# Linear attention, top-2 MoE and GLU in one kernel: remainder tokens of k and v in 1024-byte pieces, token numbers in the one-hots, two weight splits and the quarter list moved forward

## The chip, the cores and the metric

The kernel runs on one core of a Trainium2 chip, in one launch. The metric is device time in microseconds, as the median of several runs; lower is better. Engines are named as the profile names them: PE (matrix products), DVE (VectorE), ACT (ScalarE), POOL (GpSimd) and SP (the queue that issues most transfers).

## The reference

Three layers run one behind the other on 2304 tokens (4 batches of 576) of width 512 (8 heads of 64).

```python
kv = einsum('bhsd,bhse->bhde', k, v)            # 64 x 64 for each batch and head
out = einsum('bhsd,bhde->bhse', q, kv)
x = out / sqrt(mean(out * out, -1) + 1e-6) * g_norm     # then [2304, 512]

noisy = x @ w_gate + log1p(exp(x @ w_noise)) * noise    # 8 experts
top2, top2_w = two largest of noisy, softmax over the two
y[mask] += top2_w * (relu(x[mask] @ w1[e]) @ w2[e])     # F = 1024

result = (sigmoid(y @ m2_gate) * (y @ m2_val)) @ m2_out # 1536 wide, float64 weights
```

## The kernel before

**Attention.** A batch has 576 tokens: 512 "main" tokens, four neighbouring ones on each of 128 partitions (`R = 4`, pieces of 1024 bytes), and 64 remainder tokens (`SR`). `load_main` brings half of a batch's heads of k, v or q in one DMA of 512 KB; `load_rem` brings the remainder of one tensor of one batch, one token on a partition, in 512 pieces of 256 bytes (128 KB). k's remainder of two batches shares a tile; v's has one tile for each batch with zeros in the other half, so that the product over 128 partitions takes this batch alone. All these loads stand in program order in SP's queue, batch by batch: k and v of the first four heads, the remainders, k and v of the other heads, the noise, q. The small loads of `g_norm`, `w_gate` and `w_noise` are issued by ACT.

`kv_a(b)` makes the 64 x 64 products: for each of four head pairs, five steps (`R` main ones and the remainder) of two matmuls. It ends in a copy on DVE into `kvbd[b]`. `kv_b` transposes it, and `kv_c` multiplies by the gate weights times g_norm (`gwb`, which DVE makes in `early`, line 311, from `wcat` and `gcol`), so that `kvbd[b]` gives a tile's output and its gate logits in one product. For batch 0 this is done in two halves, in an order on PE that is written out by hand with filler matmuls (`warm`). Then a loop over 18 tiles of 128 tokens (`q_transpose`, `attend`) runs with `kv_a` to `kv_c` of batches 1 to 3 in it (`hooks`).

**Routing.** Tiles form four groups (`GROUPS`). `route(g)` is a generator, stepped by `advance` and `step`: it makes the norm, the logits, the two best experts (`oh`, `km`, `mk`), the rank in the expert by products on PE (`prk`), slot numbers (`sb`, `rm`), and one-hots for a list of tokens: `ohs` of the place in a block (128 wide, one instruction for each tile and choice, line 539) and `ovs` of the block (one instruction for the group, line 541, and one that multiplies it by the token numbers `tokid`, line 543). Of `ohs`, all of group 0, the second choices of groups 1 and 2 and three of the last group's five second choices are made by POOL, the others by DVE. A sum of their products is the list of tokens for each block: `pfirst` over the first two groups gives the first two blocks of expert 0 (`lsa`, two gathers on POOL), `plist` over all groups gives everything (`lsb`). `lsq` holds the same list for gathers by quarter rows, which experts 1 to 7 use.

**Experts.** The first 256 tokens of expert 0 are computed while the last two groups are still being routed: `h_first(0..3, 0)` for the hidden layer, `y_step(0, 0)` and `y_step(0, 1)` for its output. Between them `work()` splits the next piece of an expert's weights into a high part (ACT, line 644 or 647) and a low part (DVE, line 645 or 648); which `step` and which `work()` stands where is written by hand. After the list, POOL gathers blocks 2 to 4 of expert 0, DVE scales them (`xs`), PE transposes them, ACT and DVE make `xh` and `xl`, and `h_first(0..3, 1)` starts. From there expert follows expert: PE does three products for each exact one, DVE and ACT split weights and hidden values, POOL gathers and scales the next expert's rows (lines 714, 720 and 733). The GLU follows, in a table of steps made at build time. SP and POOL keep program order; PE and DVE have the order of the text where a `with in_order` says so, and a list scheduler's order elsewhere.

## Time and profile before

| | |
|---|---|
| median of 3 runs | 944.24 us (944.13 to 947.38) |
| the profiled execution | 937.66 us, of which 935.9 us are the span of instructions |
| PE busy in the span | 909.1 us (97%) |
| DVE, ACT, POOL busy | 682.3, 439.6, 383.6 us |
| transferred | 213.92 MB, 229 GB/s on average |

All rows below are of one profiled execution, which was 6.6 us shorter than the median of the plain runs. Times count from the start of the span. A share of busy time is an average over stages, so stages are looked at one by one. "Busy" of PE counts overlapping matmuls once, and its idle time is printed with the name of what ended it.

### The profile page before, as it was taken

How to read it: one execution, taken by the hardware profiler on the slowest of the kernel's cores; microseconds unless marked ns; L12 is line 12 of the kernel's file. 1: busy time of each engine (PE TensorE's matmuls, PEld its weight loads, DVE VectorE, ACT ScalarE, POOL GpSimd, SP SyncE). 2: the span in 40 equal slices, each digit the busy share in tenths (PEclk: the TensorE clock that was granted, in tenths of full speed). 3: DMA queues.
4: the chain of work that ended last, by engine and by line, in shares of the span. 5: the costliest groups of instructions: out<-in, count | busy, mean ns of one | idle time of the engine just before them, and what ended most of it. 6: DMA issues, size and time to landing. Idle time of an engine off the chain costs nothing.

```text
span 935.9 us, 14318 instructions
## 1 busy us (share of the span) xinstructions
PE 909.1 (97%) x5157; PEld 788.7 (84%) x5157; DVE 682.3 (73%) x1025; ACT 439.6 (47%) x659; POOL 383.6 (41%) x378
## 2 busy tenths in 40 slices
...
GB/s 263 290 257 216 188 216 279 259 257 274 262 188 234 185 221 194 207 206 216 225 155 141 140 251 215 217 333 222 171 266 263 244 253 252 350 269 201 217 249 98
DMA packets 134379, 213.92 MB, mean 229 GB/s; under 512 B 20384, under 2 KB 65952, under 8 KB 134304
## 3 DMA queue, kind: packets, MB, share of 16 engines
...
q14 instruction: 34, 0.28, 0.1%
...
## 4 chain that ended last, share of the span: by engine, by line
PE 58%; DVE 5%; DMA 4%; ACT 2%; issue 2%; SPq 1%; POOL 0%; DVEq 0%; ACTq 0%
PE py L817 15%; PE ph L774 14%; PE pga L1174 8%; PE poa L1353 7%; PE pgc L1174 4%; PE poc L1353 3%; PE pgb L1174 2%; PE pout L1323 2%; PE pob L1353 2%; DMA xturn<-yg 1%; DMA yg<-ybuf,slot 1%; DVE wt L994 1%; DMA lw<-wbuf 1%; DMA yg<-xturn 1%; DVE xf L1072 1%
## 5 line engine op out<-in xcount | busy, mean ns | idle before, releaser
L714 POOL DMA_INDIRECT xg<-xbuf,lsq x132 | 152.8, 1158 | 51.2 <-issue 30.9
L994 DVE TENSOR_TENSOR wt<-lw,wt 128x512 fp32r<-128x512 f32 x84 | 69.9, 837 | 35.7 <-ACT wt L993 33.6
L778 ACT ACTIVATE hh<-ph 128x624 fp32r<-128x624 f32 (+1 forms) x60 | 41.4, 694 | 95.7 <-PE ph L774 93.9
L779 DVE SCALAR_TENSOR_TENSOR hl<-ph,hh 128x624 fp32r<-128x624 f32 (+1 forms) x60 | 48.7, 811 | 48.2 <-ACT hh L778 47.0
L714 POOL DMA_INDIRECT yg<-ybuf,slot x36 | 39.0, 1084 | 77.6 <-issue 57.7
L733 POOL TENSOR_TENSOR xg<-xg 128x512 f32<-128x512 f32 x33 | 36.5, 1107 | 40.3 <-DMA xg<-xbuf,lsq 35.2
L763 ACT ACTIVATE xh<-xT 128x512 fp32r<-128x512 f32 (+3 forms) x40 | 21.1, 543 | 66.6 <-DVE xT L760 65.4
L993 ACT ACTIVATE wt<-lw 128x512 fp32r<-128x512 f32 x84 | 49.9, 621 | 0.0
L1211 POOL TENSOR_TENSOR qt<-qv 128x512 f32<-128x512 f32 x12 | 19.7, 1642 | 68.9 <-DVE qv L1198 37.2
L1188 ACT ACTIVATE q<-pga 128x1024 f32<-128x1024 f32 x24 | 24.6, 1027 | 44.8 <-PE pga L1174 43.5
L764 DVE TENSOR_TENSOR xl<-xT,xh 128x512 fp32r<-128x512 f32 (+3 forms) x40 | 24.9, 634 | 27.0 <-ACT xh L763 27.0
L695 POOL COPY seen<-hh 128x1 f32<-128x1 f32 x42 | 16.8, 401 | 65.7 <-ACT hh L778 65.5
L774 PE MATMUL ph<-xh,w_3h 128*128 128x312 f32 (+2 forms) x128 | 39.3, 307 | 1.6 <-DVE hl L779 0.9
L774 PE MATMUL ph<-xh,w_3l 128*128 128x312 f32 (+2 forms) x128 | 39.3, 307 | 1.5 <-DVE w_3l L645 1.5
L774 PE MATMUL ph<-xl,w_0h 128*128 128x312 f32 (+2 forms) x128 | 39.1, 313 | 1.3 <-DVE xl L764 1.3
L822 ACT ACTIVATE yo<-py 128x512 f32<-128x512 f32 (+1 forms) x40 | 23.5, 588 | 35.6 <-PE py L817 32.7
L774 PE MATMUL ph<-xh,w_1l 128*128 128x312 f32 (+2 forms) x128 | 39.2, 307 | 0.7 <-DVE w_1l L645 0.7
L774 PE MATMUL ph<-xh,w_0l 128*128 128x312 f32 (+2 forms) x128 | 39.6, 312 | 0.3 <-PEq L852 0.3
L774 PE MATMUL ph<-xh,w_0h 128*128 128x312 f32 (+2 forms) x128 | 39.6, 312 | 0.0
L774 PE MATMUL ph<-xh,w_1h 128*128 128x312 f32 (+2 forms) x128 | 39.2, 306 | 0.0
L774 PE MATMUL ph<-xl,w_2h 128*128 128x312 f32 (+2 forms) x128 | 39.1, 306 | 0.0
L774 PE MATMUL ph<-xh,w_2h 128*128 128x312 f32 (+2 forms) x128 | 39.1, 306 | 0.0
...
## 6 DMA issues: line engine op xcount, KB each, us to landing
...
```

The lines of the kernel that those rows point to most:

```text
L714: nc.gpsimd.indirect_dma_start(out=x, out_offset=None, in_=src, in_offset=bass.IndirectOffsetOnAxis(ap=ix, axis=0))
L733: eng.tensor_mul(xv, xv, x[:, :, 128:, None].to_broadcast([128, 4, KD, 32]))
L764: nc.vector.tensor_sub(XL[e, s][:, :, a:z], pt[:, :, o:o + z - a], XA[e, s][:, :, a:z].bitcast(FT))
L774: nc.tensor.matmul(ph, w[:, c, j], x[e, s][:, c, :], start=(n == 0), stop=(n == 3 * KD - 1))
L778: nc.scalar.activation(hh, ph, AF.Relu)
L779: nc.vector.scalar_tensor_tensor(hl, ph, 0.0, hh.bitcast(FT), op0=OP.max, op1=OP.subtract)
L817: nc.tensor.matmul(py[0:m], x[:, f % 2, t], w[:, f % 2, :], start=(n == 0), stop=(n == 3 * FC - 1))
L993: nc.scalar.activation(hi, src, AF.Copy)
L994: nc.vector.tensor_sub(lo, src, hi.bitcast(FT))
L1174: nc.tensor.matmul(ps[:, j, 0:HT[c]], w[:, a, k, s], x[:, k, :], start=(first and i == 0), stop=(i == 5), skip_group_check=not first)
L1188: nc.scalar.activation(q[name], src, AF.Copy)
L1353: nc.tensor.matmul(ps[:, j, 0:HT[c]], w, g[x][1][:, f, :], start=(first and u + f + i == 0), stop=(u == FP3 - 1 and f + i == 3), skip_grou ...
```

## The change

Six things are changed.

1. `load_rem` brings k's and v's remainder as 16 pieces of four neighbouring tokens for each head: partition 16 h + i holds tokens 4 i to 4 i + 3 of head h, in 128 pieces of 1024 bytes. A head's tokens now stand on 16 partitions only, so masks are needed: `kown` (two tiles, zeroed once) gets the 32 partitions of a head pair by four copies a batch, and `vown` is v times a 0/1 column (`own`) for even and for odd heads, two instructions a batch. DVE does these for batch 0 and POOL for batches 1 to 3. `kv_a` then runs four remainder steps of two matmuls for each head pair instead of one.
2. `load_qrem` puts the two batches of q's remainder on even and odd partitions; `attend` takes every second column of the transposed tile. The pieces stay at 256 bytes.
3. `gcol`, `w_gate` and `w_noise` are issued by SP, behind k and v of batch 0.
4. The token number is multiplied into `ohs` as a second operation of the same instruction; the separate product on `ovs` is dropped, and the last group's second choices move from POOL to DVE.
5. The splits of w1 pieces 1 and 3 of expert 0 stand before the `h_first` that they used to stand behind.
6. The quarter list is made directly behind the whole list.

```diff
-    krem, qrem = (wt([128, B // 2, H, D], FT, f"{nm}rem") for nm in "kq")
+    kown = [wt([128, HP, R * D], FT, f"kown{i}") for i in range(2)]
+    qrem = wt([128, B // 2, H, D], FT, "qrem")
...
+    krem, vown = wt([128, B, R * D], FT, "krem"), []
+    own = cst.tile([128, 2], FT, name="own")
...
-    def load_rem(dst, src, b):
-        nc.sync.dma_start(dst[64 * (b % 2):64 * (b % 2) + 64],
-                          hbm(src, b * H * S * D + SM * D, [[D, SR], [S * D, H], [1, D]]))
+    def load_rem(b):
+        vown.append(et([128, 2, R * D], FT, f"vown{b}"))
+        nc.sync.dma_start(krem[:, b], hbm(k, b * H * S * D + SM * D, [[S * D, H], [R * D, SR // R], [1, R * D]]))
+        nc.sync.dma_start(vown[b][:, 1], hbm(v, b * H * S * D + SM * D, [[S * D, H], [R * D, SR // R], [1, R * D]]))
+
+    def load_qrem(b):
+        nc.sync.dma_start(qrem[b % 2::2, b // 2], hbm(q, b * H * S * D + SM * D, [[D, SR], [S * D, H], [1, D]]))
...
-    for s in range(2):
-        nc.scalar.dma_start(gcol[64 * s:64 * s + 64, :], hbm(g_norm, 0, [[1, 64], [1, 1]]))
-    nc.scalar.dma_start(wcat[:, :, 0:E], w_gate.rearrange("(c p) e -> p c e", p=128))
-    nc.scalar.dma_start(wcat[:, :, E:2 * E], w_noise.rearrange("(c p) e -> p c e", p=128))
+    nc.sync.dma_start(gcol, hbm(g_norm, 0, [[0, 2], [1, 64], [1, 1]]))
+    nc.sync.dma_start(wcat[:, :, 0:E], w_gate.rearrange("(c p) e -> p c e", p=128))
+    nc.sync.dma_start(wcat[:, :, E:2 * E], w_noise.rearrange("(c p) e -> p c e", p=128))
...
     def kv_a(b, pairs=(0, HP)):
         a, z = pairs
+        for hp in range(a, z):
+            p = slice(32 * hp, 32 * hp + 32)
+            (nc.gpsimd if b else nc.vector).tensor_copy(kown[b % 2][p, hp], krem[p, b])
+        for s in range(2) if not a else ():
+            (nc.gpsimd if b else nc.vector).tensor_scalar(vown[b][:, s], vown[b][:, 1], own[:, s:s + 1], None,
+                                                          op0=OP.mult)
         pk = pa([128, z - a, 128], "pkv")
         for hp in range(a, z):
-            for r in range(R + 1):
+            for r in range(2 * R):
...
-                        (krem[:, b // 2, 2 * hp + s, :], vrem[b][:, 2 * hp + s, :])
+                        (kown[b % 2][:, hp, d], vown[b][:, s, d])
...
-                eng = nc.gpsimd if j and (g != len(groups) - 1 or i < 3) or not g else nc.vector
-                eng.tensor_scalar(ohs[:, i, j], i128[:, 0:128], rm[:, i, j:j + 1], None, op0=OP.is_equal)
+                eng = nc.gpsimd if j and g != len(groups) - 1 or not g else nc.vector
+                eng.tensor_scalar(ohs[:, i, j], i128[:, 0:128], rm[:, i, j:j + 1], tokid[:, t0 + i:t0 + i + 1],
+                                  op0=OP.is_equal, op1=OP.mult)
...
-                nc.vector.tensor_mul(ovs[:, :n], ovs[:, :n], tokid[:, t0:t1, None, None].to_broadcast(shp))
...
+        work()
         step(third)
-        step(last, 2)
-        work()
-        step(last)
+        step(last, 3)
         h_first(0, 0)
     work()
     step(third)
     step(last, 4)
     step(third, 2)
-    step(last)
+    work()
     h_first(1, 0)
-    step(last, 3)
+    step(last, 4)
     step(third)
-    work()
     h_first(2, 0)
...
         for blk in range(AB, NB):
             gather(0, blk)
+        lsf = sml.tile([128, NB * E], HF, name="lsf")
+        nc.vector.tensor_copy(lsf, pl)
+        psq = pa([128, 4, NB * E], "psq")
+        for b in range(4):
+            nc.tensor.matmul(psq[:, b], sel[:, b], lsf, start=True, stop=True)
+        nc.vector.tensor_scalar(lsq, psq, quarter, 4.0 * TOK, op0=OP.add, op1=OP.add)
```

What that makes of the order is shown at two places. The first is SP's queue at the start of the program. Before, two k remainders (batches 0 and 1) and one of v stand between the two halves of batch 0's k and v (a name's number tells tiles apart):

```order
L218 DMA k_128<-in_k_dram 128x4x256
L218 DMA v_130<-in_v_dram 128x4x256
L222 DMA krem<-in_k_dram 64x8x64 x2
L222 DMA vrem_156<-in_v_dram 64x8x64
L218 DMA k_129<-in_k_dram 128x4x256
L218 DMA v_131<-in_v_dram 128x4x256
```

Now:

```order
L221 DMA k_128<-in_k_dram 128x4x256
L221 DMA v_130<-in_v_dram 128x4x256
L226 DMA krem<-in_k_dram 128x1x256
L227 DMA vown_169<-in_v_dram 128x1x256
L221 DMA k_129<-in_k_dram 128x4x256
L221 DMA v_131<-in_v_dram 128x4x256
L257 DMA gcol<-in_g_norm_dram 128x1x1
L258 DMA early<-in_moe_w_gate_dram 128x4x8
L259 DMA early<-in_moe_w_noise_dram 128x4x8
```

The remainder of batch 1 has left this place, and the three small loads of `gcol` and the gate weights (the tile `early`) have come in behind the second half of k and v. On DVE, the first instructions that wait for a load stand like this before (`kvbd` is the tile of the 64 x 64 products):

```order
L311 TENSOR_SCALAR early<-early,gcol 64x4x16 x2
L278 TENSOR_SCALAR ident<-jp 128x128
L280 TENSOR_SCALAR tri<-jp 128x128
L288 TENSOR_SCALAR sel<-sel 128x512
L355 COPY kvbd_250<-pkv 64x2x64 x2
L372 COPY kvbd_250<-pgw 128x2x32
```

Now:

```order
L349 COPY kown_152<-krem 32x256 x4
L215 TENSOR_SCALAR jown<-jown 128x2
L282 TENSOR_SCALAR ident<-jp 128x128
L217 TENSOR_SCALAR own<-jown 128x2
L284 TENSOR_SCALAR tri<-jp 128x128
L351 TENSOR_SCALAR vown_169<-vown_169,own 128x256
L292 TENSOR_SCALAR sel<-sel 128x512
L351 TENSOR_SCALAR vown_169<-vown_169,own 128x256
L315 TENSOR_SCALAR early<-early,gcol 64x4x16 x2
L365 COPY kvbd_256<-pkv 64x2x64 x2
L382 COPY kvbd_256<-pgw 128x2x32
```

The masks of batch 0 have come in ahead, and `early`, which waits for the gate weights, still stands ahead of the first copy of `kvbd`.

The second place is DVE around the whole list (`lsb`), where `w_0_1l` to `w_0_3l` are the low parts of expert 0's w2 pieces. Before:

```order
L541 TENSOR_TENSOR ohv<-i_226,sb 128x10x40
L539 TENSOR_SCALAR ohv<-i_226,rm 128x128 x6
L556 TENSOR_TENSOR tw<-tw,dn 128x5
L548 SCALAR_TENSOR_TENSOR slot<-sb,rm 128x10
L539 TENSOR_SCALAR ohv<-i_226,rm 128x128
L543 TENSOR_TENSOR ohv<-ohv,tokid 128x10x40
L554 TENSOR_SCALAR dn<-dn 128x5
L648 TENSOR_TENSOR w_0_1l<-raw,w_0_1h 128x1024
L1520 TENSOR_SCALAR lsb<-plist 128x40
L555 RECIPROCAL tw<-dn 128x5
L648 TENSOR_TENSOR w_0_2l<-raw,w_0_2h 128x1024
L556 TENSOR_TENSOR tw<-tw,dn 128x5
```

Now:

```order
L553 TENSOR_TENSOR ohv<-i_232,sb 128x10x40
L550 TENSOR_SCALAR ohv<-i_232,rm,tokid 128x128 x6
L559 SCALAR_TENSOR_TENSOR slot<-sb,rm 128x10
L550 TENSOR_SCALAR ohv<-i_232,rm,tokid 128x128 x4
L567 TENSOR_TENSOR tw<-tw,dn 128x5
L659 TENSOR_TENSOR w_0_2l<-raw,w_0_2h 128x1024
L1529 TENSOR_SCALAR lsb<-plist 128x40
L1533 CAST lsf<-plist 128x40
L659 TENSOR_TENSOR w_0_3l<-raw,w_0_3h 128x1024
L1537 TENSOR_SCALAR lsq<-psq,quarter 128x160
```

The product by `tokid` is gone, ten one-hots of the last group stand where seven stood, one more split (`w_0_2l`) stands ahead of `lsb`, and the quarter list (`lsf`, `lsq`) has moved up to it.

## Rows read from the trace of the kernel before

**Rows 1.** Busy time by stage; columns: stretch, engines' busy us, PEclk, DMA share, GB/s.

```profile
20.00:54.00 34.00, 29.83 (x408) 27.34 (x409) 16.72 (x56) 21.84 (x52) 4.21 (x4) 1.00 1.10 295
...
136.00:536.00 400.00, 397.93 (x2261) 359.20 (x2260) 306.80 (x435) 161.65 (x239) 195.75 (x199) 1.00 0.66 216
```

**Rows 2.** Timeline of PE: start us, us, instruction; in brackets the idle time before.

```profile
7.12 0.69 PE L352 MATMUL pkv<-v,k 128*64 128x64 f32 x16 [0.62 <-DMA v<-in_v_dram]
...
20.60 1.35 PE L410 MATMUL po<-kvbd,qT 128*128 128x160 f32 x8
...
48.37 0.69 PE L352 MATMUL pkv<-v,k 128*64 128x64 f32 x16
48.88 0.29 PE L352 MATMUL pkv<-vrem,krem 128*64 128x64 f32 x4
```

**Rows 3.** Waits of PE, 18 to 70 us: us in total, times, longest.

```profile
PE pkv L352 <- DMA v<-in_v_dram: 3.0, 2, 1.6
PE pkv L352 <- PE pqT L395: 0.9, 1, 0.9
PE prk L497 <- DVE mk L492: 0.8, 1, 0.8
PE pfirst L1432 <- POOL ohv L539: 0.6, 2, 0.4
```

**Rows 4.** DMA view, 0 to 54 us: GB/s in 40 slices, then queues (packets, MB, share).

```profile
GB/s 0 9 292 338 280 155 83 375 353 323 349 349 352 289 225 335 337 345 336 203 284 338 257 133 149 338 344 329 350 347 350 297 178 344 325 354 338 244 203 291
...
q10 hardware_dynamic: 1216, 0.03, 1.6%
```

**Rows 5.** Timeline of DVE, the first kv product.

```profile
9.44 0.52 DVE L311 TENSOR_SCALAR early<-early,gcol 64x64 f32<-64x64 f32 x2 [5.92 <-DMA vrem<-in_v_dram]
...
11.21 0.59 DVE L355 COPY kvbd<-pkv 64x128 f32<-64x128 f32 x2 [0.68 <-PE pkv L352]
```

**Rows 6.** Timeline of PE, the end of attention.

```profile
69.56 3.60 PE L1482 MATMUL warm<-qT 128*128 128x512 f32 x8
```

**Rows 7.** Groups of instructions of POOL, 0 to 110 us.

```profile
L539 POOL TENSOR_SCALAR ohv<-i,rm 128x128 f16<-128x128 f16 x21 | 17.5, 846 | 19.2 <-DVE rm L530 14.8 <-DVE ohv L541 4.4
```

**Rows 8.** Timeline of DVE, the routing of the last group.

```profile
78.31 1.28 DVE L645 SCALAR_TENSOR_TENSOR w_1l<-raw,gcol,w_1h 128x1024 fp32r<-128x1024 f32 x1 [1.25 <-ACT w_1h L644]
...
94.71 0.56 DVE L543 TENSOR_TENSOR ohv<-ohv,tokid 128x400 f16<-128x400 f16 x1
```

**Rows 9.** Timeline of DVE, the list and the first split behind it.

```profile
97.25 0.20 DVE L1520 TENSOR_SCALAR lsb<-plist 128x40 int32<-128x40 f32 x1 [0.77 <-PE plist L1432]
...
117.09 3.73 DVE L645 SCALAR_TENSOR_TENSOR w_0l<-raw,gcol,w_0h 128x1024 fp32r<-128x1024 f32 x1 [0.18 <-ACT w_0h L644]
```

**Rows 10.** Waits of PE, 70 to 150 us.

```profile
PE ph L774 <- DVE w_3l L645: 1.5, 1, 1.5
PE py L817 <- DVE hl L779: 1.4, 1, 1.4
...
PE plist L1432 <- POOL ohv L539: 1.3, 1, 1.3
PE ph L774 <- DVE hl L779: 0.9, 1, 0.9
PE ph L774 <- DVE w_1l L645: 0.7, 1, 0.7
```

**Rows 11.** Timeline of PE, the second half of expert 0.

```profile
109.47 0.43 PE L774 MATMUL ph<-xl,w_0h 128*128 128x368 f32 x1 [1.06 <-DVE xl L764]
...
110.08 0.51 PE L774 MATMUL ph<-xl,w_0h 128*128 128x368 f32 x1
...
113.80 0.33 PE L774 MATMUL ph<-xh,w_0l 128*128 128x368 f32 x1
```

**Rows 12.** Timeline of POOL, gathers behind the list.

```profile
107.97 0.94 POOL L714 DMA_INDIRECT xg<-xbuf,lsq  x1 [2.94 <-DVE lsq L1540]
...
117.65 2.08 POOL L720 TENSOR_TENSOR xs<-xg 128x512 f32<-128x512 f32 x2
```

37 lines of the change are left out of this document (15 added, 22 removed).

## The prediction

> **What bounds the kernel now.** I read the busy time by stage first. From 136 us to 536 us PE is busy 397.93 of 400 us [rows 1], and behind the routing of the last tokens no instruction is changed, so that the rest moves as a block: only the first 136 us can gain or lose. In the attention stage, 20 to 54 us, PE is busy 29.83 of 34 us while the DMA engines are full (share 1.10) [rows 1]. So two resources are near their limit there, and the change gives to one (loads) and takes from the other (PE). The timeline of PE shows the first tile's product at 20.60 us and the kv product of batch 3 running without a gap from 48.37 us [rows 2]; the waits of PE show what stops it: 3.0 us for v in two waits and 0.9 us at the start of batch 1's kv product, which I also take for a load, then 0.8 us for a mask and 0.6 us for POOL's one-hots [rows 3]. The DMA view shows a plateau of some 350 GB/s with dips to 155 and 83 (6.8 to 9.5 us) and 133 to 149 (31 to 34 us) where 256-byte pieces are moved [rows 4]. After attention, the view that counts is the chain from the last group's routing to the list, `lsb`, at 97.25 us, and from there to the second half of expert 0.
>
> **1. Loads.** The 38 slices of 1.35 us from 2.7 us on average 293 GB/s; at 350 they would be over 8.4 us sooner [rows 4]. Eight of the twelve remainder loads get large pieces, two pairs of q's keep theirs; I take 5 us as gained on the last load. That alone is no time: PE waits only 3.0 + 0.9 us for loads [rows 3], and no more than that can come back.
>
> **2. The start.** The gate weights go behind 4 x 512 KB + 2 x 128 KB = 2.36 MB, 6.7 us at 350 GB/s, from 2.7 us on: 9.4 us. Their 1152 small pieces cost 11.4 ns each (1.6% of 54 us x 16 engines over 1216 packets [rows 4]), 0.8 us over 16 engines. The lag from last byte to reader is about 1.4 us: 1.05 MB from 2.7 us ends at 5.7, and the first product starts at 7.12 [rows 2]. So DVE can begin `early` near 11.7 us instead of 9.44, and the first `kvbd` copy, in order behind it, comes near 12.3 instead of 11.21 [rows 5]: +1.1. The first half's added matmuls lie beside this wait; the second half's (0.8, below) are on the path; the 0.9 us wait falls away. The first tile comes 1.0 us later. Bounds: -0.9 if the gate weights are no later, +4 if they land 3 us later than taken.
>
> **3. PE.** 16 records of a main pair take 48.88 - 48.37 = 0.51 us, 4 of the remainder a quarter of it, 0.13 [rows 2]. The remainder becomes 16: +0.38 for a pair, 1.5 us a batch, 4.6 us for batches 1 to 3. Against that fall the waits for v (3.0), for the mask and for POOL (0.8 and 0.6) [rows 3], since the same scheduler now puts the mask ahead of a copy and two products by `tokid` leave DVE: -4.4. I take a further 0.4 off for those two products. End of attention on PE, 69.56 us now [rows 6]: +1.0 + 4.6 - 4.4 - 0.4 = **+0.8**. The masks on POOL, six instructions of 256 columns a batch, lie between half and twice the 0.85 us that POOL's one-hot of 128 columns takes [rows 7]; near it they are 5 us a batch, and POOL is busy 4.21 of these 34 us [rows 1], so I take nothing; without that cover, batch 1 alone could cost 2 us, since its remainder lands closest to its use. Bounds of this part: -3 (PE finds time for the matmuls in waits) to +4.
>
> **4. The list.** DVE is the bound from 74 to 97 us; I sum its queue. Gone: 1.25 us of waiting for `w_1h` [rows 8], because the split now stands earlier; 0.77 us of waiting for `plist` [rows 9], whose last factor came from POOL (PE waits 1.3 us for it [rows 10]); two `tokid` products of 0.5 [rows 8]. Added: three one-hots, 0.5; one more split ahead of `lsb` in the new order, 1.2 (as the 1.28 of [rows 8], less overlap); 0.4 for a norm that ACT now does behind a split. Sum -0.9. PE's own waits for `w_3l` and `w_1l`, 1.5 + 0.7 [rows 10], go too, but hide behind the list: PE ends its first blocks sooner and waits for the gathers. Behind the gathers, five small counting instructions stand ahead of `xl` on DVE now (+0.5), and `lsq` no longer does (-0.4). Second half of expert 0, first `xl` product at 109.47 [rows 11]: **-0.8**. Bounds: -2.0 (a wait of PE was the bound) to +0.5 (the extra split costs what the rest gives).
>
> **5. The clock.** Matmuls there go 0.51 us long at 110.08 and 0.33 us at 113.80 [rows 11]: PE had waited several times from 106 us, and for 3.4 us the granted clock is at the lower of its two levels; 11 matmuls lose 0.15 each, 1.7 us. PE will idle longer ahead of this point, so the low stretch should come earlier and lie half beside the idle time: **-0.8**. Bounds: -1.7 (all beside) to +1.7 (two such stretches).
>
> **6. Behind the list.** POOL waits 2.94 us for `lsq`, starts expert 1's quarter gathers at 107.97, and scales two blocks at 117.65 for 2.08 us [rows 12]. In that time DVE's split `w_0l` takes 3.73 us [rows 9] instead of 1.28, as if it stood behind POOL; the next loads wait for its buffer, and PE pays 0.9 and 1.4 us later [rows 10]. With `lsq` ready some 9 us sooner, POOL starts these gathers when it ends the others, about 3 us earlier, and the scaling is over as the split begins: **-1.9** of the 2.3. Bounds: -2.3 to +0.5 (POOL meets another instruction instead).
>
> Sum: +0.8 - 0.8 - 0.8 - 1.9 = -2.7. The profiled execution took 937.66 us, so 935.0; the median of plain runs stood 6.6 us above it, so 944.24 - 2.7 = **941.5 us**. 0.5% is 4.7 us, about what a measurement of this kernel can tell from no change.
>
> **A rule that speaks against it.** In this kernel's rows every load has 64 or 128 as its outermost count, and the queue keeps all 16 engines at work (share 1.10 [rows 1]). The new k and v remainders have 8 heads outermost. The Trainium skill (DMA: Bandwidth & Descriptors, "Why a DMA increments its semaphore by 16 and not by 1") says that a transfer is split over the largest number of engines up to 16 that divides both sides' outermost counts; by that, these eight loads run on 8 engines, and `gcol`, with 2 outermost, on 2. No row of before shows such a load; worked out from rows it is the second rival.
>
> **Rivals.** *Attention follows its loads* (faster): PE's added matmuls find their place in waits that the names of the rows do not show, and the end of attention moves by -3 instead of +0.8. For it: PE is 4.2 us idle in 20 to 54 us and the loads come 5 us sooner. Against it: the gap-free stretches of PE. 941.5 - 3.8 = 937.7. *Half the engines*: a remainder pair is 256 pieces; an engine moves 1024 bytes in 47 ns at 350 GB/s over 16, so the pair takes 32 x 47 ns = 1.5 us of 8 engines instead of 0.75 of 16, 0.75 us a batch for all that queues behind. If that and POOL's masks behind it keep the 3.0 us of waits for v alive, the time is 944.5. *Late gate weights* (slower): every tile stands behind `kvbd` of batch 0, and that on DVE behind `early`. If small pieces at the end of a full queue land 4 us later than I took (15.7 instead of 11.7), the first tile is 4 us later, all of attention with it, and the time is 945.5; it decides from 2.7 us on. The old trace has a sign of it: a wait of 5.92 us for loads ahead of `early` [rows 5]. That the change would not do what it says is seen in one place: `lsb` stands behind one more split, which is in the sum.
>
> **How the numbers follow.** The forecast, 0.44; attention follows its loads, 0.26; half the engines, 0.17; late gate weights, 0.13. The range 936.5 to 946.5 takes in all four centres and leaves the last tenth on either side to sums of bounds. Faster by over 0.5% (under 939.5): nearly all of the first rival and a little of the forecast, 0.28. Slower by over 0.5% (over 949.0): half of the late weights, 0.07. Within: 0.65.
>
> **What would show it.** Right: no wait of PE for v from 20 to 54 us, GB/s without the dips at 7 to 9 and 31 to 34 us, the first tile near 21.6 us, filler at the end of attention near 70.4, `lsb` near 97.1 with no wait for POOL, quarter gathers near 105, `w_0l` under 2 us, and no waits of PE of 0.9 and 1.4 us near 125 and 135 us. Wrong: `early` on DVE past 14 us; waits of PE for POOL's masks in batch 1; a start of the second half of expert 0 at or behind 109.5; POOL's scaling beside another split.

## The result and the profile after

| | |
|---|---|
| before, median of 6 runs | 945.81 us (944.13 to 948.82) |
| changed, median of 6 runs | 957.81 us (954.84 to 961.88) |
| ratio | 1.0132, 95% interval 1.0103 to 1.0162 |
| forecast | 941.5 us, range 936.5 to 946.5 |
| profiled execution, changed | 960.37 us, of which 958.1 us are the span |

The changed kernel is 1.3% slower, some 12.5 us. The profile of before is of an execution that was short for its kernel, so the two spans (958.1 and 935.9) are 22 us apart, and only part of that is the change. Where the 22 us arise is read from places that both programs pass, each a row of the timeline of PE (the list: of DVE):

| place, us from the start | before | changed | difference |
|---|---|---|---|
| first tile's product | 20.60 | 23.53 | +2.9 |
| end of attention on PE | 69.56 | 79.33 | +9.8 |
| list `lsb` | 97.25 | 106.17 | +8.9 |
| second half of expert 0, first `xl` product | 109.47 | 120.35 | +10.9 |
| expert 1, first hidden product | 147.07 | 158.20 | +11.1 |
| GLU, first `pgv` product | 533.79 | 545.11 | +11.3 |
| GLU, first `pga` product | 572.09 | 594.22 | +22.1 |

By the first product of expert 1 some 11 us are lost, most of them by the end of attention, and they stay up to the GLU. The other 10.8 us lie between `pgv` and `pga` (49.1 us instead of 38.3); run 1 below shows 47.8 us there for the unchanged kernel, so they belong to the execution.

Busy time by stage of the changed kernel, with the columns of [rows 1]:

```profile
20.00:54.00 34.00, 29.90 (x412) 27.52 (x410) 13.30 (x29) 18.69 (x43) 14.41 (x22) 0.95 1.07 300
...
70.00:110.00 40.00, 37.11 (x247) 30.40 (x248) 32.33 (x118) 19.13 (x37) 15.17 (x18) 0.91 0.42 139
110.00:136.00 26.00, 20.66 (x105) 18.98 (x103) 12.71 (x26) 8.85 (x11) 21.76 (x21) 0.80 0.70 208
```

and the two middle stages of before:

```profile
70.00:110.00 40.00, 33.32 (x235) 26.72 (x234) 31.77 (x108) 16.38 (x29) 17.61 (x20) 1.00 0.59 186
110.00:136.00 26.00, 23.66 (x125) 21.94 (x124) 20.92 (x23) 13.19 (x15) 18.57 (x19) 0.93 0.74 224
```

In attention PE is as busy as before (29.90 us of 34, 29.83 in [rows 1]), and its clock is 0.95 instead of 1.00; run 17 below, a later profile of the unchanged kernel, has 0.95 there too. From 70 to 110 us it is 0.91 and from 110 to 136 us 0.80, where before had 1.00 and 0.93. The DMA engines are at 0.42 instead of 0.59 from 70 to 110 us, since the list and its gathers come later.

**The start.** SP's queue of the changed kernel (start us, us on the queue):

```profile
5.10 3.72 SPq L258 DMA_DIRECT2D early<-in_moe_w_gate_dram  x1
8.87 1.33 SPq L259 DMA_DIRECT2D early<-in_moe_w_noise_dram  x1
...
12.21 1.13 SPq L221 DMA_DIRECT2D q<-in_q_dram  x2
```

The load of `w_gate` keeps the queue for 3.72 us, those of `w_noise` and the noise behind it 1.33 us each, so that q of batch 0 is issued at 12.21 us. In the profile of before q went at 9.88, and SP's queue had stood for 3.3 us in two waits that the profile puts down to `gcol`'s load on ACT's queue (3.2 us in run 2, 3.3 in run 4 below): the queue was held in both orders. The DMA view, 0 to 54 us in 40 slices of 1.35 us, has the hole that follows:

```profile
GB/s 0 14 302 376 291 212 287 222 68 16 109 384 361 347 353 241 216 326 343 341 321 301 308 279 291 247 290 311 335 347 338 312 260 268 291 272 320 347 259 328
```

The dips that [rows 4] had at 31 to 34 us are gone, as forecast; but from 10.8 to 14.9 us the rate is 68, 16 and 109 GB/s, which [rows 4] did not have. `early` on DVE comes at 12.40 us, not 11.7 as forecast (9.44 in [rows 5]):

```profile
12.40 0.52 DVE L315 TENSOR_SCALAR early<-early,gcol 64x64 f32<-64x64 f32 x2 [1.91 <-DMA early<-in_moe_w_noise_dram]
```

On PE the first tile then waits behind a kv product of batch 1 that is in order ahead of it and whose v is late:

```profile
23.30 0.30 PE L362 MATMUL pkv<-v,k 128*64 128x64 f32 x2 [2.47 <-DMA v<-in_v_dram]
23.53 2.31 PE L422 MATMUL po<-kvbd,qT 128*128 128x160 f32 x8
```

The first tile is at 23.53 us (20.60 in [rows 2]), and behind the wait of 2.47 us it runs at the lower of the two clock levels: 2.31 us for eight matmuls instead of 1.35. The wait alone does not settle the clock, since run 9 below, the same program up to here, waited as long and kept the higher level:

```profile
23.55 0.30 PE L362 MATMUL pkv<-v,k 128*64 128x64 f32 x2 [2.56 <-DMA v<-in_v_dram]
23.78 1.35 PE L422 MATMUL po<-kvbd,qT 128*128 128x160 f32 x8
```

Batch 3's kv product is at 54.06 us, 5.7 us later than in [rows 2]. 1.6 us of that are a new wait of PE, for the copy of batch 2's kv product. On DVE this copy now stands behind two instructions for the gate logits (`Lr`, `lg`, 0.8 us each), ahead of which it stood before:

```profile
45.55 0.82 DVE L480 TENSOR_REDUCE lg<-Lr 128x80 f32<-128x640 f32 x1
46.28 0.85 DVE L365 COPY kvbd<-pkv 64x256 f32<-64x256 f32 x2
```

```profile
47.19 0.66 PE L373 MATMUL pkvT<-ident,kvbd 128*128 128x128 f32 x4 [1.64 <-DVE kvbd L365]
```

**The end of attention.** POOL's one-hots, duration of one (min/median/max), before and after:

```profile
L539 POOL TENSOR_SCALAR ohv<-i,rm x21: 590/612/2310, 56.5 to 94.7; 128x128 f16<-128x128 f16 x21
```

```profile
L550 POOL TENSOR_SCALAR ohv<-i,rm,tokid x18: 784/832/1786, 61.0 to 96.7; 128x128 f16<-128x128 f16 x18
```

Two operations in one instruction take 832 ns instead of 612. Thirteen of them stand in a row ahead of the first list: 11.44 us instead of 9.05. PE's waits from 18 to 150 us (us in total, times, longest):

```profile
PE pxT L767 <- issue: 2.6, 1, 2.6
PE pkv L362 <- DMA v<-in_v_dram: 2.5, 1, 2.5
PE pfirst L1443 <- POOL ohv L550: 2.1, 4, 0.6
PE ph L785 <- DVE hl L790: 1.8, 1, 1.8
```

PE waits 2.1 us for these one-hots (0.6 in [rows 3]). The timeline shows what is behind the wait:

```profile
72.47 0.19 PE L1443 MATMUL pfirst<-ohv 128*128 128x2 f16 x1 [0.56 <-POOL ohv L550]
...
72.98 2.34 PE L422 MATMUL po<-kvbd,qT 128*128 128x160 f32 x8
...
75.97 3.52 PE L422 MATMUL po<-kvbd,qT 128*128 128x160 f32 x16
```

The last three tiles, one of which stood between the first list's products before, now come behind them, and run at the lower clock: eight `po` matmuls take 2.34 us, where run 9 has 1.25 for the same eight. Runs 4, 5, 9, 13 and 14 below have the same four waits, 2.1 to 2.2 us in all; behind them the clock fell in runs 4 and 13 and stayed full in runs 5, 9 and 14.

**Behind the list.** The list comes 26.84 us after the end of attention instead of 27.69, 0.85 us less, about what was forecast; but runs 9 and 14, the same program up to the list, have 27.62 and 27.81 us there, so a gain is not shown. From the list to the first `xl` product it is 14.18 us instead of 12.22. PE waits 1.3 and 2.6 us there for the gathered blocks, the third of which DVE scales 9.82 us behind the list (8.46 in the profile of before), and the second half starts at the lower clock:

```profile
121.13 0.51 PE L785 MATMUL ph<-xh,w_0h 128*128 128x368 f32 x1
```

Up to 126 us 20 matmuls are slow, 0.51 us or longer instead of 0.33 (11 in the profile of before, [rows 11]); a matmul starts every 0.307 us in that stretch and every 0.167 behind it. On DVE:

```profile
130.10 1.28 DVE L656 SCALAR_TENSOR_TENSOR w_0l<-raw,gcol,w_0h 128x1024 fp32r<-128x1024 f32 x1 [0.18 <-issue]
131.30 2.07 DVE L656 SCALAR_TENSOR_TENSOR w_1l<-raw,gcol,w_1h 128x1024 fp32r<-128x1024 f32 x1
```

The split `w_0l` takes 1.28 us instead of 3.73, as forecast. But `w_1l`, and `w_2l` and `w_3l` behind it, take 2.07 each, beside three scalings on POOL (131.21 us, 5.07 us), and the next hidden value makes PE wait 1.8 us.

### The profile page after: what moved, and what is told of

Its sections match the earlier page's. It is cut to its first block, busy times and chain, and to the rows that moved or that the text cites. A ratio compares the mean times of both kernels' runs of the same rounds, so it can differ in the third digit from the quotient of the medians.

```text
span 958.1 us, 14716 instructions
## 1 busy us (share of the span) xinstructions
PE 926.2 (97%) x5347; PEld 802.6 (84%) x5349; DVE 683.3 (71%) x1031; ACT 441.1 (46%) x659; POOL 394.9 (41%) x393
## 3 DMA queue, kind: packets, MB, share of 16 engines
HBM read 140.94 MB, written 71.97 MB: 222 GB/s over the span
## 4 chain that ended last, share of the span: by engine, by line
PE 75%; DVE 8%; DMA 6%; issue 3%; SPq 3%; ACT 2%; POOL 1%; another core or an unknown queue 1%; DVEq 0%; POOLq 0%; ACTq 0%
PE ph L785 19%; PE py L828 17%; PE pga L1185 13%; PE poa L1364 7%; PE pgc L1185 6%; PE poc L1364 3%; PE pgb L1185 3%; PE pgv L1153 2%; PE pout L1334 2%; PE pob L1364 2%; DMA v<-in_v_dram 2%; DMA raw<-in_moe_w_dram 1%; POOL ohv L550 1%; DMA krem<-in_k_dram 1%; SPq L221 1%
## 5 line engine op out<-in xcount | busy, mean ns | idle before, releaser
L1153 PE MATMUL pgv<-x0h,w 128*128 128x256 f32 x192 | 39.4, 298 | 1.4 <-issue 1.4
L785 PE MATMUL ph<-xh,w_2l 128*128 128x312 f32 (+2 forms) x128 | 39.2, 306 | 0.3 <-DVE w_2l L656 0.3
```

The costliest lines, as they stand in the source:

```text
L785: nc.tensor.matmul(ph, w[:, c, j], x[e, s][:, c, :], start=(n == 0), stop=(n == 3 * KD - 1))
L1153: nc.tensor.matmul(pg[:, k // 2, 0:PC], w[:, a, d, s], X0[x][:, 2 * (k % 2) + d, :], start=(k % 2 == 0 and d + a + x == 0), stop=(k % 2 == ...
```

## The experiments

Two theories stood at first: the **start** (the gate loads in SP's queue, with the added matmuls) and the **one-hots** on POOL with the clock behind them. Ratios are to the kernel before on the same chip; the kernel before itself took 944.7 to 946.3 us on the chip of runs 1 to 8 and 938.5 to 939.7 on those of runs 9 to 18, so times are compared on one chip only. The quotient of two medians differs a little from the ratio, and lies in its interval each time. Runs 9 and 14 are one kernel on one chip and gave 1.0061 and 1.0105, so 0.4% between two runs can come without any change. The places of all runs, in us (run 12 is a single execution):

| run | ratio (95%) | first tile | attention ends | list | first `xl` | expert 1 |
|---|---|---|---|---|---|---|
| 1 before again | 0.9989 (0.9957 to 1.0020) | 20.90 | 70.02 | 97.62 | 110.08 | 147.68 |
| 17 before again | 0.9998 (0.9971 to 1.0026) | 20.89 | 71.37 | 100.15 | 112.61 | 149.56 |
| 2 parts 1, 2 | 1.0027 (1.0005 to 1.0049) | 24.71 | 72.96 | 99.47 | 111.53 | 148.57 |
| 3 part 3 | 0.9995 (0.9968 to 1.0021) | 22.88 | 71.27 | 98.87 | 111.45 | 149.02 |
| 5 part 4 | 1.0041 (1.0020 to 1.0061) | 20.93 | 72.03 | 99.41 | 112.77 | 150.76 |
| 6 part 5 | 1.0026 (1.0002 to 1.0050) | 20.71 | 69.59 | 97.56 | 111.52 | 149.12 |
| 7 part 6 | 1.0019 (0.9996 to 1.0042) | 21.21 | 69.56 | 98.57 | 111.09 | 149.75 |
| 4 all but 3 | 1.0097 (1.0060 to 1.0135) | 24.36 | 75.82 | 103.50 | 117.34 | 159.75 |
| 8 all but 4 | 1.0076 (1.0043 to 1.0108) | 23.57 | 74.95 | 101.60 | 115.09 | 151.07 |
| 13 changed again | 1.0114 (1.0078 to 1.0150) | 23.34 | 79.05 | 105.82 | 119.87 | 157.28 |
| 9 changed, filler | 1.0061 (1.0038 to 1.0085) | 23.78 | 75.96 | 103.58 | 116.18 | 149.82 |
| 14 changed, filler | 1.0105 (1.0067 to 1.0142) | 23.77 | 76.98 | 104.79 | 117.27 | 151.24 |
| 10 parts 1, 2 repaired | 0.9985 (0.9963 to 1.0007) | 22.16 | 71.97 | 99.75 | 111.86 | 145.24 |
| 11 part 4, last group | 0.9977 (0.9952 to 1.0002) | 21.04 | 69.48 | 97.83 | 109.73 | 143.12 |
| 18 part 4, last group | 0.9962 (0.9940 to 0.9985) | 20.85 | 69.98 | 97.73 | 109.82 | 143.19 |
| 12 run 2, 16 outermost | | 23.17 | 71.41 | 99.37 | 111.22 | 144.60 |
| 15 runs 10 and 11 | 1.0013 (0.9988 to 1.0038) | 21.16 | 71.86 | 98.80 | 110.90 | 147.98 |
| 16 run 11, filler | 0.9997 (0.9970 to 1.0025) | 21.05 | 69.86 | 99.13 | 110.85 | 144.96 |

**Run 1: the kernel before again** (no edit).

> The kernel before, unchanged, profiled once more. Its first profile was 6.6 us under the median of its plain runs, and the changed kernel's profile lost 11.3 us up to the entry of the GLU (545.1 us against 533.8 for the first pgv product) and 10.8 us more between that and the first pga product (49.1 us against 38.3). Theory 'entry': that second loss is not the change's; executions differ there, and this profile will again show some value between 38 and 50 us there, with all places up to 533 us within 1 us of the first profile. Rival 'change': the entry takes 38.3 us again, as nothing is changed, and the loss belongs to the change. Ratio 1.000 either way.

Measured: places up to 533 us within 0.7 us of the first profile, and 47.8 us from `pgv` to `pga`. "Entry" holds: that loss is not the change's. Run 17 below limits the first half of the sentence: a third execution is 1.8 to 3.1 us later from the end of attention on, so a single profile's place says nothing under some 3 us.

**Run 2: parts 1 and 2 alone.**

```diff
+        nc.sync.dma_start(krem[:, b], hbm(k, ..., [[S * D, H], [R * D, SR // R], [1, R * D]]))
...
+            for r in range(2 * R):
...
```

> The kernel before with parts 1 and 2 alone (remainders of k and v in large pieces, masks, 24 more matmuls in each half of a kv product; q's remainder on odd and even partitions). Theory 'queue' (the loss at the start is the gate loads in SP's queue): first tile near 20.6 us or up to 1 us sooner, no wait of PE for v over 1 us, end of attention 69.6 to 71.5, time 942 to 947. Rival 'remainder' (the added matmuls, 1.4 us a batch, and POOL's masks lie on the path): end of attention at 73 or later and a time of 948 or more.

Measured: 1.0027, slower by some 2.6 us (0.0027 of 946); the first tile is at 24.71 us, though the gate loads are on ACT. So the forecast of neither theory for the start holds. Waits of PE for v are gone, as "queue" said. What is late is on DVE:

```profile
11.19 0.53 DVE L316 TENSOR_SCALAR early<-early,gcol 64x64 f32<-64x64 f32 x2 [1.68 <-DMA early<-in_moe_w_noise_dram]
...
12.17 0.35 DVE L352 TENSOR_SCALAR vown<-vown,own 128x256 f32<-128x256 f32 x1
```

and PE, whose remainder matmuls need `vown`:

```profile
12.57 1.48 PE L363 MATMUL pkv<-vown,kown 128*64 128x64 f32 x15 [4.02 <-DVE vown L352]
```

In this order `early`, which waits for the gate weights (11.19 us here), stands ahead of both of v's masks, and PE waits 4.02 us. The place of the mask in DVE's order, not its work (0.35 us), makes the first tile late. The end of attention, 72.96 us, is 0.04 short of what "remainder" said, and the time (949.95) in its range.

**Run 3: part 3 alone.**

```diff
-    nc.scalar.dma_start(wcat[:, :, 0:E], w_gate.rearrange("(c p) e -> p c e", p=128))
...
+    nc.sync.dma_start(wcat[:, :, 0:E], w_gate.rearrange("(c p) e -> p c e", p=128))
...
```

> The kernel before with part 3 alone (the loads of g_norm, w_gate and w_noise issued by SP behind k and v of batch 0, in place of ACT). Theory 'queue': the issue of w_gate's load keeps SP 3 to 4 us as in the changed kernel (3.72), the rate falls under 50 GB/s for 2 us or more near 11 to 14 us, and the first tile is 2.5 to 4 us later than 20.60, the end of attention 2 to 4 us later, time 946 to 950. Rival 'not alone': the queue has room here since the remainders are in it for longer, the first tile is under 1.2 us later and the time is within 2 us of before.

Measured: the mechanism is there, on SP's queue:

```profile
8.04 2.18 SPq L254 DMA_DIRECT2D early<-in_moe_w_noise_dram  x1
```

(`w_noise` 2.18 us, q at 11.85), with a rate of 58 and 11 GB/s from 11 to 13 us; the first tile is 2.3 us late and the end of attention 1.7, both a little under the range of "queue", and the latter no later than in run 17, the kernel before. The time is that of before, 0.9995 (946.71 us, which both ranges allow). So a first tile that is 2 us late costs nothing that a run can tell here.

**Run 4: all but part 3.**

```diff
+    nc.scalar.dma_start(wcat[:, :, 0:E], w_gate.rearrange("(c p) e -> p c e", p=128))
...
-    nc.sync.dma_start(wcat[:, :, 0:E], w_gate.rearrange("(c p) e -> p c e", p=128))
...
```

> The changed kernel with part 3 undone (those three loads on ACT again). Theory 'queue': SP issues q of batch 0 from 8 to 9 us instead of 12.2, no stretch under 50 GB/s, first tile at 20 to 21 us instead of 23.5, end of attention 75 to 77 instead of 79.3 (what stays is the remainder's matmuls, slower one-hots on POOL and the low clock behind them), time 952 to 955 against 957.8 of the changed kernel. Rival 'remainder': kv products wait for masks and matmuls all the same, end of attention within 1.5 us of 79.3 and the time within 2 us of the changed kernel.

Measured: q at 8.80 us and an end of attention at 75.82, both as "queue" said; the first tile is at 24.36, as in run 2, after 4.4 us in which PE waited for v's mask. The time is 1.0097, against 1.0132 for the whole change, with intervals that overlap. What it won by the end of attention, 3.5 us, is lost behind the list, where 36 matmuls of expert 0 are at the lower clock and the split `w_0l` takes 4.39 us beside POOL's scalings.

**Run 5: part 4 alone.**

```diff
-                eng.tensor_scalar(ohs[:, i, j], i128[:, 0:128], rm[:, i, j:j + 1], None, op0=OP.is_equal)
+                eng.tensor_scalar(ohs[:, i, j], i128[:, 0:128], rm[:, i, j:j + 1], tokid[:, t0 + i:t0 + i + 1],
+                                  op0=OP.is_equal, op1=OP.mult)
...
```

> The kernel before with part 4 alone (token number as a second operation in each one-hot, no product on the block one-hots, the last group's second choices on DVE). In the changed kernel POOL's one-hot takes 832 ns (median) instead of 612, thirteen stand in a row ahead of the first list, and PE's order has more of the first list's products ahead of the last tiles. Theory 'one-hot': thirteen one-hots end 2.4 to 3 us later than in the kernel before, PE waits 1.5 to 2.5 us for POOL there, and then runs at the lower clock; end of attention 73 to 75.5 instead of 69.6, time 948 to 951 (+3 to +5). Rival 'harmless': the second operation costs under 0.1 us, end of attention within 1 us of before, and the time is the same or up to 2 us less, by the product left out.

Measured: 1.0041, +3.9 us. PE waits 2.1 us for the one-hots, and thirteen take 11.02 us instead of 9.05 (787 ns for one by the median, 832 in the changed kernel). "One-hot" holds in place and price; the low clock does not show here (1.00 from 70 to 80 us), and the end of attention is 72.0, a little under its range.

**Run 6: part 5 alone.**

```diff
+        work()
         step(third)
-        step(last, 2)
-        work()
-        step(last)
+        step(last, 3)
...
```

> The kernel before with part 5 alone (splits of w1 pieces 1 and 3 of expert 0 moved ahead). Theory 'one-hot': neutral or a gain, PE's waits for w_3l and w_1l (1.5 and 0.7 us) are gone, the list 0 to 1 us sooner, time -2 to +1. Rival 'splits': the list is 1 us or more later, since one more split stands ahead of it, and the next weights are loaded later: time +2 to +4.

Measured: 1.0026. Neither theory named the cause. The waits for `w_3l` and `w_1l` are gone and the list is where it was (97.56 us), but PE, with its work done sooner, now waits 3.6 us for the gathered blocks, and its clock is 0.87 and 0.62 in the two stretches from 100 to 120 us (1.00 in both in run 1):

```profile
108.10 1.09 PE L756 MATMUL pxT<-ident,xs 128*128 128x128 f32 x4 [2.44 <-DVE xs L720]
```

The hole has two causes. One is the work that moved ahead of the list. The other is the gather: DVE scales the third block 9.70 us behind the list, 8.46 in the profile of before. Run 6, then before:

```profile
107.26 0.69 DVE L720 TENSOR_TENSOR xs<-xg 128x512 f32<-128x512 f32 x1 [2.31 <-DMA xg<-xbuf,lsb]
```

```profile
105.71 0.69 DVE L720 TENSOR_TENSOR xs<-xg 128x512 f32<-128x512 f32 x1 [1.63 <-DMA xg<-xbuf,lsb]
```

It is 9.5 to 9.8 us in all seven profiles of kernels with part 5 and 8.1 to 9.1 in all others, though POOL issues the third gather 3.8 to 3.9 us behind the list in both kinds. With part 5 the block so lands some 1 us later; why is open. Behind the hole 21 matmuls are slow.

**Run 7: part 6 alone.**

```diff
+        lsf = sml.tile([128, NB * E], HF, name="lsf")
+        nc.vector.tensor_copy(lsf, pl)
...
```

> The kernel before with part 6 alone (quarter list directly behind the whole list). Theory 'gathers collide' (the quarter gathers of expert 1 now follow those of expert 0 without a pause and share the DMA engines with them and with weights): the third block of expert 0 is scaled 9.5 us or more behind the list instead of 8.5, the second half starts later, time +1 to +3. Rival 'as forecast': quarter gathers 2 to 3 us sooner, POOL's scaling is over before the split of w_0l, which takes under 2 us instead of 3.73, time -1 to -2.5.

Measured: 1.0019, not clearly slower, and no gain. The third block is scaled 8.6 us behind the list, so "gathers collide" does not hold for this part. `w_0l` takes 1.28 us, as forecast; the collision with POOL (a scaling of 2.06 us from 124.19 on) has moved to `w_3l`, ahead of a hidden value that PE waits for:

```profile
120.35 1.28 DVE L645 SCALAR_TENSOR_TENSOR w_0l<-raw,gcol,w_0h 128x1024 fp32r<-128x1024 f32 x1 [0.18 <-ACT w_0h L644]
...
123.94 3.40 DVE L645 SCALAR_TENSOR_TENSOR w_3l<-raw,gcol,w_3h 128x1024 fp32r<-128x1024 f32 x1
```

```profile
128.23 0.62 PE L774 MATMUL ph<-xh,w_3h 128*128 128x368 f32 x1 [2.18 <-DVE hl L779]
```

**Run 8: all but part 4.**

```diff
...
+                nc.vector.tensor_mul(ovs[:, :n], ovs[:, :n], tokid[:, t0:t1, None, None].to_broadcast(shp))
```

> The changed kernel with part 4 undone (one operation in each one-hot, the product on the block one-hots, three of the last group's second choices on POOL). Theory 'one-hot': PE waits under 1 us for the first list, no low clock behind it, end of attention 74 to 76.5 instead of 79.3, time 951 to 954 (-4 to -7 from the changed kernel). Rival 'start' (the late loads and the added matmuls carry it all): end of attention 78 or later, time within 2 us of the changed kernel.

Measured: 1.0076, and the end of attention at 74.95 instead of 79.33: "one-hot" again, in its range. Half of these 4.4 us are the last three tiles, at the full clock here.

**Runs 9, 13 and 14: fillers behind the list.**

```diff
+        pf = pa([128, 512], "fill")
         for blk in range(AB, NB):
+            for _ in range((0, 5, 11)[blk - AB]):
+                nc.tensor.matmul(pf, sel[:, 0], sel.rearrange("p b i -> p (b i)"), start=True, stop=True)
             expert_in(0, blk)
...
```

> The changed kernel with filler matmuls behind the list (19 products of 512 columns whose result nobody reads, 5 ahead of the second block's transposes, 11 ahead of the third's, 3 ahead of the second half of expert 0), 4.1 us of PE at full clock, in a stretch where PE waited 1.3 + 2.6 + 0.6 us and then ran 20 matmuls of the second half at the lower clock, 0.14 us longer each. Theory 'clock' (idle time of PE behind the list, made longer by the parts that moved work ahead of it, costs twice: once as a wait and once by the clock behind it): no or few slow matmuls, second half done 2 to 3 us sooner, time -2 to -3 from 957.8. Rival 'wait alone' (the third block's gather sets the time, the clock is an accident): the same time within 1 us, or later by the fillers.

> The changed kernel once more, on the same chip as the next run, since the plain kernel took 938.5 us on the chip of runs 9 to 12 and 944.7 to 946.3 on that of runs 1 to 8. Theory 'clock': 1.3% slower than the kernel before again, or less where fewer of its matmuls run at the lower clock; the low stretch behind the list (118 to 126 us in its first profile) is there again. Rival 'chip': the ratio is 1.006 as in run 9, and the fillers of run 9 gave nothing.

> The kernel of run 9 (the changed kernel with 19 filler matmuls behind the list) beside the changed kernel on one chip. Theory 'clock': 3 to 7 us less than run 13. Rival 'chip': within 2 us of run 13.

Run 9 gave 1.0061, but on another chip than the first comparison. Side by side on that chip, the changed kernel (run 13) took 947.45 us and the one with fillers (run 14) 946.22; the intervals overlap nearly whole, so by the times "chip" was right about the gain (not about the ratio, 1.0114 instead of 1.006) and "clock" wrong by its range. The profiles show why. Stages of run 13, 110 to 130 us:

```profile
110.00:120.00 10.00, 4.96 (x24) 3.34 (x22) 4.49 (x13) 2.34 (x4) 7.57 (x8) 0.78 0.75 221
120.00:130.00 10.00, 10.00 (x44) 10.00 (x45) 3.63 (x12) 3.24 (x4) 8.29 (x9) 0.70 0.70 222
```

and of run 14:

```profile
110.00:120.00 10.00, 9.47 (x53) 6.26 (x52) 5.78 (x21) 2.34 (x4) 7.72 (x8) 1.00 0.85 263
120.00:130.00 10.00, 10.00 (x65) 9.90 (x63) 7.58 (x6) 6.46 (x7) 8.43 (x8) 1.00 0.75 247
```

The clock is full with fillers (1.00 for 0.78 and 0.70), no matmul of the second half is slow (21 were), and expert 1 starts 6.0 us sooner, 2.1 of which were there at the end of attention already. At the first hidden product of expert 3 it is only 2.3 us (265.27 against 267.58). Run 14 has there a wait for an output copy, and then the lower clock once more:

```profile
258.06 0.48 PE L828 MATMUL py<-w_0h,hh 128*112 128x512 f32 x1 [1.90 <-ACT yo L833]
...
259.22 0.63 PE L828 MATMUL py<-w_0l,hh 128*112 128x512 f32 x1
```

In run 13 this wait is 0.54 us, with no slow matmuls behind. What PE gains early is in part waited away at 258 us.

**Run 10: parts 1 and 2, with `early` made by POOL.**

```diff
-        nc.vector.tensor_scalar(gwb[p, :, 2 * E * s:2 * E * (s + 1)], wcat[p], gcol[p], None, op0=OP.mult)
+        nc.gpsimd.tensor_scalar(gwb[p, :, 2 * E * s:2 * E * (s + 1)], wcat[p], gcol[p], None, op0=OP.mult)
...
```

> Run 2 (parts 1 and 2 alone) with one thing changed: the product of the gate weights with g_norm is made by POOL, behind its zeroing of kvbd, so that the masks of batch 0 don't stand behind it on DVE. Theory 'queue of DVE' (in run 2 PE waited 4.0 us for v's mask, since DVE waited for the gate weights with the mask behind it): that wait is under 2 us, the first tile 1.5 to 3 us sooner than 24.7, end of attention 70 to 72 instead of 73.1, time -1 to -2.5 from run 2. Rival 'matmuls' (the 1.4 us of added matmuls a batch carry the loss): end of attention within 0.7 us of 73.1.

Measured: the first tile is at 22.16 us, 2.6 sooner than in run 2, and the end of attention at 71.97, so "queue of DVE" holds for the start; the wait is still 3.0 us, not under 2. The ratio is 0.9985 instead of 1.0027, but that is not shown to come from the start: the list is at 99.75 us, 0.3 later than in run 2, and the 3.3 us at expert 1 are won behind it, where `w_0l` takes 1.28 us instead of 3.80 (see runs 11 and 18).

**Runs 11 and 18: part 4 for the last group alone.**

```diff
+                if g == len(groups) - 1:
+                    eng.tensor_scalar(ohs[:, i, j], i128[:, 0:128], rm[:, i, j:j + 1], tokid[:, t0 + i:t0 + i + 1],
+                                      op0=OP.is_equal, op1=OP.mult)
...
```

> The kernel before with part 4 for the last group alone (its ten one-hots on DVE, with the token number; the other groups as before, POOL with one operation). Theory 'POOL pays' (what cost in part 4 is the second operation on POOL, ahead of the first list): end of attention within 0.6 us of 69.6 to 70.2, no wait for POOL ahead of the list, list up to 0.7 us sooner, time -1.5 to +0.5. Rival 'DVE pays': the ten one-hots make the list 0.5 us or more later, time +1 to +3.

> Run 11 once more (token number in the last group's one-hots alone), since its interval ended at 1.0002. Theory 'worth something': ratio 0.996 to 0.999 again. Rival 'nothing': 0.999 to 1.002, as with the fillers in run 16, since a wait for yo near 258 us, which the kernel before has too, takes back what comes early.

Measured, on two chips: 0.9977 (0.9952 to 1.0002) and 0.9962 (0.9940 to 0.9985): a little faster than before, and so than the changed kernel. "POOL pays" holds: with one operation in POOL's instructions as before, the rest of part 4 is a small gain. But not where it was looked for: the list is not sooner (97.83 and 97.73). Expert 1 starts at 143.1 and 143.2 us instead of 147.1 to 149.6: from the first `xl` product it is 33.4 us in both runs and 37.0 to 37.6 in the three profiles of before. What differs there is how the splits meet POOL. Run 1, DVE and POOL:

```profile
117.63 3.83 DVE L645 SCALAR_TENSOR_TENSOR w_0l<-raw,gcol,w_0h 128x1024 fp32r<-128x1024 f32 x1 [0.18 <-issue]
```

```profile
118.29 2.07 POOL L720 TENSOR_TENSOR xs<-xg 128x512 f32<-128x512 f32 x2
```

Run 18, DVE and POOL:

```profile
115.89 1.28 DVE L650 SCALAR_TENSOR_TENSOR w_0l<-raw,gcol,w_0h 128x1024 fp32r<-128x1024 f32 x1 [0.18 <-ACT w_0h L649]
117.09 1.28 DVE L650 SCALAR_TENSOR_TENSOR w_1l<-raw,gcol,w_1h 128x1024 fp32r<-128x1024 f32 x1
118.28 2.08 DVE L650 SCALAR_TENSOR_TENSOR w_2l<-raw,gcol,w_2h 128x1024 fp32r<-128x1024 f32 x1
```

```profile
118.01 3.26 POOL L725 TENSOR_TENSOR xs<-xg 128x512 f32<-128x512 f32 x2
```

In run 1 the split `w_0l` begins 0.66 us ahead of POOL's scaling, and the split pays: 3.83 us instead of 1.28, the scaling 2.07. In run 18 one split is over and the second nearly so when the scaling begins, at 118.01 us; that and the two splits behind it share the loss (3.26, and 2.08 and 2.07), and PE waits for none of them. The Trainium skill (SBUF — State Buffer, "Who interferes with whom") says that the two engines share a port pair, and that the instruction issued first holds it while the other is blocked. That they slow each other these rows show. Who was first does not settle it: in run 1 the split was first and paid all of it, in run 18 the split that was first kept its 1.28 us, and in run 6 the scaling was first (119.75 us, 2.07) and the split paid (120.34 us, 2.57). Why the first hidden value is ready earlier in run 18 (its ReLU starts at 113.96 us, in run 1 at 115.70, with the first `xl` product 0.26 us apart) was not found.

**Run 12: remainder with 16 outermost.**

```diff
-        nc.sync.dma_start(krem[:, b], hbm(k, ..., [[S * D, H], [R * D, SR // R], [1, R * D]]))
+        nc.sync.dma_start(krem[:, b], hbm(k, ..., [[R * D, SR // R], [S * D, H], [1, R * D]]))
```

> Run 2 with the loads of k's and v's remainder written with 16 outermost (four tokens' piece, then the head) instead of 8 (the head, then the piece), so that the pieces land on other partitions than the masks take them from: sizes, counts and engines of all instructions are as in run 2, but the output is not that of the reference. Theory 'half the engines': in run 2 these loads keep 8 of 16 engines and the rate near them is 226 to 284 GB/s; now 330 or more there, and the second half of batch 0 lands sooner. Rival 'pieces': the same dips to 230 to 280 GB/s, since they come from something else than the outermost count.

Measured: the DMA view from 5.9 to 9.7 us of run 2 (busy share of the engines in 40 slices in tenths, GB/s, then the totals):

```profile
DMA  4552389999999999999999999999999979999999
GB/s 108 76 86 65 90 146 188 280 315 348 368 367 350 312 329 235 274 255 277 293 260 259 249 265 155 193 278 255 281 216 226 226 151 259 280 345 356 366 316 323
DMA packets 1833, 0.95 MB, mean 251 GB/s; under 512 B 929, under 2 KB 1833, under 8 KB 1833
```

and of run 12:

```profile
DMA  6666988999999999999999999999999999999999
GB/s 194 207 186 160 198 215 213 261 273 311 291 265 307 333 307 382 348 346 270 270 334 323 356 323 366 328 282 297 317 244 276 244 233 284 282 295 313 280 280 323
DMA packets 2177, 1.08 MB, mean 283 GB/s; under 512 B 1159, under 2 KB 2177, under 8 KB 2177
```

283 GB/s instead of 251, and three slices under 250 in the second half of the stretch where run 2 had seven: the direction of "half the engines", but not its 330. The share is 0.9 or more in both in that half, so idle engines are not what these rows show. In run 12 `early` comes at 10.14 us and the first tile at 23.17, 1.1 and 1.5 us sooner than in run 2, more than the 0.3 us by which the first tile differs between the profiles of before on two chips. But run 12 is one execution on another chip than run 2, so the rule of the Trainium skill that the prediction weighed is made likelier and not shown; PE waited for no load in either.

**Runs 15 and 16: can the parts be put together?**

> The kernel before with the parts that gave something once repaired: run 10 (remainders in large pieces, gate weights' product on POOL) and run 11 (token number in the last group's one-hots alone, all on DVE) together. Theory 'parts add': ratio 0.994 to 0.998, that is 2 to 5 us faster than before. Rival 'first tile': the remainder's masks still make the first tile 1.2 us later and the added matmuls fill what the loads gave: ratio 0.998 to 1.001, no better than run 11.

> Run 11 (token number in the last group's one-hots alone) with 6 filler matmuls behind the list, 3 ahead of the third block's transposes and 3 ahead of the second half of expert 0, 1.3 us of PE at full clock. Theory 'clock': the low stretch that the first profile of before had at 110 to 113 us doesn't come, and what a late DVE start costs behind it falls away: ratio 0.993 to 0.998. Rival 'no idle time left': the fillers lie on the path, ratio 0.999 to 1.002.

Run 15 has the edits of runs 10 and 11, run 16 that of run 11 and six fillers:

```diff
+            for _ in range((0, 0, 3)[blk - AB]):
+                nc.tensor.matmul(pf, sel[:, 0], sel.rearrange("p b i -> p (b i)"), start=True, stop=True)
```

1.0013 and 0.9997: neither is better than before. In the profile of run 15 the 11 slow matmuls and a `w_0l` of 3.73 us are there again, as in the first profile of before. Gains of this size did not add here; that the meeting of POOL and DVE behind the list decides it is likely and not shown.

**Run 17: the kernel before on another chip** (no edit).

> The kernel before, unchanged, profiled a third time, to have a profile of it from the chip of runs 9 to 16 if this call lands there. Theory: if the kernel before takes 938 to 940 us here, the places of its first profile come again within 1 us up to 533 us (first tile 20.6 to 21.2, end of attention 69.6 to 70.2, list 97.2 to 97.8), and the entry of the GLU takes 38 to 41 us; the loss of run 13 is then 9 to 10 us up to the second expert and stays. Rival: places differ by over 2 us from chip to chip ahead of the list too, and the comparison of profiles across calls is void. Ratio 1.000 either way.

Measured: 939.6 us, ratio 0.9998; 40.5 us from `pgv` to `pga`. End of attention 71.37 and list 100.15 are 1.8 and 2.9 us later than in the first profile, so the rival is right about the list: single profiles differ by that much. Run 13 against the three profiles of before is still 7.7 to 9.5 us later at the end of attention, 7.7 to 10.2 at expert 1.

## Why the prediction was wrong

**What bounds the kernel.** Right that only the first 136 us matter: the 11.1 us at expert 1 are 11.3 us at the GLU. Too simple in "moves as a block": an early PE waits near 258 us (run 14), the 4 us that runs 11 and 18 are ahead at expert 1 are 0.9 and 4.3 at the GLU (532.90 and 529.45 against 533.79 us), and the GLU's entry takes 38 to 49 us from execution to execution.

**Loads (step 1).** Right: large pieces take out the dips, and with the gate loads on ACT (runs 2 and 4) PE waits for no v at all. In the whole change one wait of 2.5 us stays, by the hole that part 3 makes.

**The start (step 2).** +1.0 forecast, +2.9 measured. I priced the small loads by their packets (0.8 us over 16 engines) and not by their time on SP's queue, 3.72 + 1.33 + 1.33 us, which holds back all that stands behind; that SP had stood 3.3 us there before is no part of my sum either. That is the rival of the late gate weights, with the place right and the cause another; alone it costs nothing that run 3 could tell.

**PE in attention (step 3).** The failing step: +0.8 for the end of attention, +9.8 measured (7.7 to 9.5 in run 13, against three profiles of before), outside my bound of +4. The added matmuls were sized right: batch 3's kv product begins 5.7 us later and ends 7.1 later, 1.4 us against 1.5. The 3.0 us of waits for v fell as I had said. They lay within the kv products of batches 1 and 2,

```profile
24.88 0.69 PE L352 MATMUL pkv<-v,k 128*64 128x64 f32 x16 [1.61 <-DMA v<-in_v_dram]
38.46 0.69 PE L352 MATMUL pkv<-v,k 128*64 128x64 f32 x16 [1.41 <-DMA v<-in_v_dram]
```

and with the added matmuls in their place these two take 4.58 and 4.12 us, 4.39 and 4.18 before; the wait for the mask is gone as well. What failed is the rest of the -4.4, and what I had not in the sum:

- The wait for POOL's one-hots, -0.6 in the sum, grew to 2.1 us, because I left out that POOL's one-hots get the second operation too: 13 x 0.22 us = 2.9 by the medians, 2.4 measured.
- The first tile comes 2.9 us later instead of 1.0, and loses another 1.0 us to the lower clock behind its wait.
- PE waits 1.6 us for the copy of batch 2's kv product, which the new order on DVE puts behind the gate logits.
- The last three tiles lose 2.2 us to the lower clock: from the last one-hot to the end of attention it is 6.8 us, and 4.6 in runs 9 and 14, where this stretch was at full clock.

The two losses to the clock, 3.2 us, are not in every execution: of runs 9 and 14, the same program up to the list, the first has neither and the second only that of the first tile. With the end of attention at 75.96 and 76.98 us they are still 4.6 to 7.4 us later than the profiles of before. What sets the clock there is open. POOL's masks, which I took for covered at 5 us a batch, take 3.6 us and were nearly on the path: at full clock, in run 9, PE waited 1.2 us for them in batches 1 and 2. By the single parts the end of attention moves by 3.4 (parts 1, 2), 1.7 (3) and 2.5 us (4) against the first profile; but the third profile of before is 1.8 us later itself, so no single one of these is clear of that, and only their times (1.0027 and 1.0041) say that parts 1, 2 and 4 cost something.

**The list (step 4).** Not shown. The -0.9 for the list came out as -0.85 against the first profile, but runs 9 and 14 have the old distance. The term itself was -0.8 for the first `xl` product, and in the first profiles that comes 1.1 us later against the end of attention: from the list to it the changed kernel takes 14.05 and 14.18 us, the kernel before 12.22 to 12.46. I had PE wait for the gathers at no cost; that the third block would land some 1 us later with part 5 (run 6) was not in the sum.

**Clock and collisions (steps 5 and 6).** -2.7 forecast; behind the list the whole change lost some 2 us up to the first `xl` product and won none of it back. I wrote that the low stretch would come earlier and lie beside the idle time. It grew instead (20 matmuls for 11), behind a hole that the moved work and the later gather made (run 6). `w_0l` is 1.28 us as forecast, but the collision went to the next splits (run 7), the case at the end of my bounds. With fillers the stretch from `xl` to expert 1 is 33.97 us (run 14), 3.6 less than the 37.60 of before; run 1 has 37.60 there with no slow matmul, so the clock is not all of it, and `w_0l` at 2.20 us instead of 3.73 is the other difference that the rows show.

**The forecast's sign.** Parts alone cost 2.6, -0.5, 3.9, 2.5 and 1.8 us (ratio less 1, by 945); their sum, 10.3, is near the 12.5 of the whole, but each has an interval of some 2 us either way, so this may be chance. No part gave a gain that a run could tell.
